# k and v with four neighbouring tokens on a partition, k^T v as 128x64 products, values as four 64x64 products at a time

## The chip, the core and the metric

The kernel runs on one core of one Trainium2 chip. The core has five engines that run their own instruction streams and wait for each other by semaphores: TensorE (matrix products; in the profile PE, and PEld for its weight loads), VectorE (DVE), ScalarE (ACT), GpSimd (POOL) and SyncE (SP, which here only issues transfers). Sixteen DMA engines move data between the memory of the chip and the core's own. The metric is the time of one execution on the device in microseconds; lower is better. Three executions of the kernel before are given, with their median.

## What is computed

Two blocks follow each other. The first is an attention without softmax, for 8 batches, 8 heads, 576 tokens and heads of 64 numbers. The second sends each of the 4608 tokens to one of eight experts.

```python
kv = np.einsum('bhsd,bhse->bhde', k, v)
out = np.einsum('bhsd,bhde->bhse', q, kv)
rms = np.sqrt(np.mean(out * out, axis=-1, keepdims=True) + 1e-06)
x = out / rms * g_norm          # then (batch, head, token, d) -> (batch*token, head*d)
...
do_compute = (x @ w_skip) > 0
e_idx = argmax(x @ w_gate);  gate_w = softmax's value there
y = gate_w * (relu(x @ w1[e_idx]) @ w2[e_idx])
out = x + y   where do_compute, else x
```

All numbers are float32. So for each batch and head a 64x64 matrix k^T v is summed over 576 tokens, and each token's q is multiplied with it.

## The kernel before

The work is in two stages. The attention stage writes x to the output tensor and finds out which expert each token needs. The expert stage gathers the tokens of one expert after another, runs the two layers, and scatters the results.

**Tokens on partitions.** `load` (L99 to L103) brings one batch of k, v or q into a tile of 128 partitions. Partition p of the lower half holds the nine neighbouring tokens 9p to 9p+8 of the even heads, the upper half those of the odd heads: `(j a) (p c) d -> (a p) j (c d)` with a = 2 and c = C = 9. A load is one DMA with pieces of 2304 bytes. `load_kv(b)` issues k and v of a batch, `load_q(b)` its q, all on the SP queue. There are three buffers for each.

**k^T v.** `state(b, third)` (L283) makes the eight heads' 64x64 sums. It runs in three thirds, each put at another place in TensorE's order. In each third six steps (u, c) are made: u is the half of the heads (four each), c the piece of nine tokens. A step is four products of 64 rows by 64 columns, one in each quarter of the TensorE array: a picks the upper or lower rows, w the left or right columns. All go to `sum_ps`, in which a is the PSUM bank. After the last third ScalarE copies the sums to `kvn`. `state_t` and `state_m` work out what w_gate and w_skip make of k^T v (nine further columns, G), so that a product with q gives logits as well; `state_s` makes `kvs`, a copy with the halves of the partitions swapped.

**Units.** The attention loop (L713) has 36 units. A unit is 256 tokens of one batch (i = 0 or 1) for one half u of the heads; the 64 tokens of a batch that are left (the ninth of each nine) are put together for four batches in units of their own (i = None). For each unit, in this order:

- `turn(n)` (L344) turns q with four TensorE transposes into `q_ps`, and ScalarE copies that to `qT`. For the left units `turn_8` does it beside other units.
- `values(n)` (L376) multiplies qT with kvn or kvs into `o_ps`, of which there are two buffers. In a usual unit eight products of 64 rows by 128 columns are made, two at a time (r is the half of the rows). In a left unit the columns too are cut in two (hf), with sixteen products of 64 by 64, four at a time. Each has 73 moving columns: 64 of k^T v and nine for the logits. TensorE needs two passes for a float32 product, which the profile records as two matmuls.
- ScalarE squares into `sq` (L398); VectorE sums the squares, `rs` (L406, `squares`); ScalarE takes the root (L413, `root`); VectorE inverts it (L420) and multiplies o_ps by it into `xl` (L423, `norm`); GpSimd adds logits and multiplies by g_norm (`finish`, L456); stores go out on the GpSimd and SP queues.

**Order.** The loop is written out by hand (`tc.manual_schedule`). In step n come turn(n+1), root(n-1), values(n), norm(n-1), squares(n); then what was put down for this step with `at`: the parts "pe" (thirds of `state` and what follows it for a batch four units ahead, L705), "late" (the routing) and "end" (loads of k and v three batches ahead and q two ahead, L706 to L709).

**Routing.** When the first 16, 26 and 36 token tiles are done, `choose`, `rank` and `number` (VectorE, with a few products) find each token's expert and slot. These stand in VectorE's order between the norms of the units.

**Start.** Loads of k, v and q of batch 0, then k and v of 1 and 2 and q of 1 (L669 to L673) go out on SP, while ScalarE's queue loads w_gate, w_skip and g_norm in six small transfers (L119 to L128). Then the parts of `state` for batch 0 run, with turn(0) after `state_t`, and the loop starts.

Of the kernel before, what the change touches and what calls it, by code (L numbers as in the profile page):

```python
# [7 lines left out]
FP32 = mybir.dt.float32  # L8
# [8 lines left out]
def kernel(  # L17
# [31 lines left out]

    nc = tc.nc
    B, H, S, D = q.shape
    DM = H * D
    N = B * S
    P = 128
    C = S // 64
    CT = 4
    NQ = 2
    NF = B // 4  # L60
    FQ = 4 * NQ + 1
# [6 lines left out]
    CAP = 384  # L68
# [3 lines left out]
    NCOL = E * CK  # L72
    ROUNDS = N // CAP
    RSPACE = 8192
    assert H == 8 and D == 64 and S == 64 * C and C == 2 * CT + 1 and B == 4 * NF and N == CAP * ROUNDS
    assert N + CAP <= RSPACE and DM == DC * 128 and NT * P == N

    keep = ctx.enter_context(tc.tile_pool(name="keep", bufs=1))
# [4 lines left out]
    kv_pool = attn.enter_context(tc.tile_pool(name="kv", bufs=3))  # L83
    q_pool = attn.enter_context(tc.tile_pool(name="q", bufs=3))
# [12 lines left out]

    kts, vts, qts = {}, {}, {}

    def load(pool, tag, src, b):  # L100
        t = pool.tile([P, 4, C, D], FP32, tag=tag, name=tag)
        nc.sync.dma_start(out=t[:, :, :, :].rearrange("p j c d -> p j (c d)"),
                          in_=src[b].rearrange("(j a) (p c) d -> (a p) j (c d)", a=2, c=C))  # L103
        return t

    def load_kv(b):
        if b < B:
            kts[b] = load(kv_pool, "k", k, b)
            vts[b] = load(kv_pool, "v", v, b)

    def load_q(b):
        if b < B:
            qts[b] = load(q_pool, "q", q, b)

    order = tc.manual_schedule()
    order.__enter__()
# [6 lines left out]
    for a in range(2):  # L123
        nc.scalar.dma_start(out=gcol[a * 64:(a + 1) * 64, :],
                            in_=g_norm.rearrange("(e o) -> e o", o=1))
# [76 lines left out]
    for w in range(2):  # L202
        nc.vector.tensor_copy(out=swap[:, w * 64:(w + 1) * 64],
                              in_=ident[:, (1 - w) * 64:(2 - w) * 64])
# [4 lines left out]
    for a in range(2):  # L209
        r = slice(a * 64, (a + 1) * 64)  # L210
# [15 lines left out]
    for lo, m in kinds:  # L226

        t = keep.tile([P, P], FP32, name=f"again{lo}_{m}")
# [43 lines left out]
    sum_ps = ps_kv.tile([P, 2, 512], FP32, name="sum_ps")[:, :, 0:2 * D].rearrange("p a (u d) -> p a u d", u=2)  # L272
# [9 lines left out]

    def state(b, third):  # L283

        kt, vt = kts[b], vts[b]
        for i in range(6 * third, 6 * third + 6):
            u, c = divmod(i, C)
            for w in range(2):
                for a in range(2):
                    r = slice(a * 64, (a + 1) * 64)  # L290
                    nc.tensor.matmul(  # L291
                        out=sum_ps[w * 64:(w + 1) * 64, a, u, :],
                        lhsT=kt[r, 2 * u + w, c, :], rhs=vt[r, 2 * u + w, c, :],
                        start=(c == 0), stop=(c == C - 1), skip_group_check=True)
        if third < 2:
            return
        kvn = kvn_pool.tile([P, 2, PK], FP32, tag="kvn", name="kvn")
        nc.scalar.copy(out=kvn[:, :, G:G + 2 * D].rearrange("p u (a d) -> p a u d", a=2), in_=sum_ps)
        kvns[b] = kvn
# [76 lines left out]
    def values(n):  # L376
        _, b, i, u = units[n]
        qT = qTs.pop(n)
        ps = ps_o.tile([P, 2, 512], FP32, tag="o", name="o_ps")

        done = turn_8(b, u, ps) if i == 0 else None
        for w in range(2):
            for a in range(2):
                cols = slice((2 * w + a) * KD, (2 * w + a + 1) * KD)
                for hf in range(1 if i is not None else 2):
                    for r in range(2):
                        rows = slice(r * 64, (r + 1) * 64)
                        if i is not None:
                            bb, to, lhsT = b, slice(0, P), qT[rows, w, a, :]
                        else:  # L390
                            bb, to = 4 * b + 2 * hf + r, slice(hf * 64, (hf + 1) * 64)
                            lhsT = qT[rows, w, hf, a * 64:(a + 1) * 64]
                        kv = kvns[bb] if w == r else kvss[bb]
                        nc.tensor.matmul(out=ps[to, r, cols], lhsT=lhsT,  # L394
                                         rhs=kv[rows, u, a * KD:(a + 1) * KD],
                                         start=True, stop=True, skip_group_check=True)
        sq = att_pool.tile([P, 2, 2, 2 * D], FP32, tag="sq", name="sq", bufs=2)
        nc.scalar.activation(out=sq[:, :, :, :], in_=heads(ps, G, G + 2 * D), func=ACT.Square)  # L398
        if done:
            done()  # L400
        ops[n] = (ps, sq)
# [276 lines left out]
    for b in range(KNOWN // S // 4 * 4, KNOWN // S):  # L678
        nc.gpsimd.dma_start(
            out=out[b * S:(b + 1) * S, :].rearrange("(p c) d -> p c d", c=C)[:, C - 1, :],  # L680
            in_=zero[:, :])
# [20 lines left out]
    for b, n in starts.items():  # L702
        if b:
            for i, part in enumerate(parts):
                at(max(n - 6 + i, (0, 0, 1, 1, 2, 3)[i]), "pe", lambda b=b, part=part: part(b))  # L705
        def loads(b=b):  # L706
            load_kv(b + 3)
            load_q(b + 2)
        at(n, "end", loads)  # L709

# [57 lines left out]
    with tc.tile_pool(name="wpool_b", bufs=2, reuse_waits="tile") as wpool_b, \  # L768
# [197 lines left out]
        rows, src = slot_rows(slice(0, NCOL), slot_pool, "")  # L966
# [37 lines left out]
        with tc.For_i(1, n_rounds, 1):  # L1004
# [8 lines left out]
                out=left[:, :].rearrange("p (r c) -> p r c", c=CK),  # L1013
# [38 lines left out]
```

## Time and profile before

| | us |
|---|---|
| three executions | 455.43, 453.71, 454.67 |
| median | 454.67 |
| the profiled execution | 461.48 |
| its span, first to last instruction | 459.6 |
| busy: TensorE / its weight loads | 400.7 / 284.0 |
| busy: VectorE / ScalarE / GpSimd | 131.4 / 94.1 / 118.4 |

The profile is of one execution, taken apart from the three. Its mean granted TensorE clock is 0.915 of full speed: in some stretches the clock was cut to one half. The costliest groups of the attention stage on TensorE are these (busy time is the union of overlapping instructions, so two groups that run at once each show it):

| line, what | records | busy us |
|---|---|---|
| L394 values, o_ps with kvn | 256 | 41.3 |
| L394 values, o_ps with kvs (at the same time) | 256 | 40.4 |
| L394 values, left units, kvn and kvs (at the same time) | 64 each | 4.7 each |
| L291 k^T v, sum_ps | 1152 | 27.4 |
| L353 transposes of q, q_ps | 128 | 24.1 |

The transfers concerned are 8 loads each of k, v and q of 1152 KB, with a median of 13.1, 13.8 and 14.9 us from issue to landing.

How to read the views that are used below. The page shows the span in 40 equal slices; a digit is the busy share of an engine in that slice in tenths, PEclk the granted clock, DMA the share of the sixteen engines. The chain of waits goes back from the last instruction: at each point it names the work that had to end for the next to start, with start, length and count. In the timeline and in the list of windows each line has a start or a stretch in us from the span's start. "x16" counts records. "64*128" is the part of the array that a product fills (rows by columns), "64x73" the moving operand.

### The profile page before, as it was taken

Reading aid. Unit: us, or ns where it says so; the run is one execution under the profiler, and the core shown is the slowest. Engines: PE = TensorE matmul, PEld = TensorE weight load, DVE = VectorE, ACT = ScalarE, POOL = GpSimd, SP = SyncE. Lnnn points to the kernel's source line nnn. Section 1 sums busy time; section 2 is a strip of 40 time slices with the busy share of each in tenths; the row PEclk is TensorE's granted clock in tenths of the full one; section 3 lists DMA queues with packets and bytes.
Section 4 is the critical chain, followed back from the end, with each engine's and each line's share of the span. In section 5 each row is a group of like instructions: output and inputs, shape, how many; then the busy total and the mean of one; then the engine's idle time right before and its main releaser. Section 6 shows DMA issues by size and latency. Waiting matters only on the chain.

```text
span 459.6 us, 8262 instructions
## 1 busy us (share of the span) xinstructions
PE 400.7 (87%) x3495; PEld 284.0 (62%) x3495; DVE 131.4 (29%) x357; ACT 94.1 (20%) x220; POOL 118.4 (26%) x185
## 2 busy tenths in 40 slices
PE   0789998998755894799999999999999999999980
PEld 0688787786645853675654764674764765856730
DVE  3132566679787552111011010110010011010010
ACT  1253574545342110010210110020110110201100
POOL 2014477444539167502001100100100101001010
PEclk9995998899675786799999999999999999999995
DMA  7899997963459999532541614425523600001000
GB/s 233 337 392 388 384 342 296 296 256 95 93 175 334 309 403 371 165 134 113 181 141 64 216 22 191 151 73 199 185 78 150 210 0 24 25 1 46 0 23 21
DMA packets 32777, 81.79 MB, mean 178 GB/s; under 512 B 3326, under 2 KB 3330, under 8 KB 32736
## 3 DMA queue, kind: packets, MB, share of 16 engines
q1 hardware_dynamic: 26656, 66.59, 41.4%
q0 software_dynamic: 4576, 14.54, 9.3%
q8 instruction: 29, 0.48, 0.4%
q10 hardware_dynamic: 1504, 0.08, 0.2%
q14 instruction: 12, 0.10, 0.1%
HBM read 66.87 MB, written 14.61 MB: 177 GB/s over the span
## 4 chain that ended last, share of the span: by engine, by line
PE 74%; DVE 13%; DMA 4%; issue 2%; ACT 2%; another core or an unknown queue 1%; POOL 0%; DVEq 0%; ACTq 0%; POOLq 0%
PE hps L888 29%; PE yps L899 27%; PE o_ps L394 6%; PE sum_ps L291 3%; PE q_ps L353 3%; DVE xl L423 3%; DMA q<-in_q_dram 2%; DVE oha_k L555 2%; PE xp L869 2%; DVE rs L406 2%; PE g_ps L320 2%; DMA wraw<-in_moe_w_gate_dram 1%; DVE bv L571 1%; DVE xt L872 1%
## 5 line engine op out<-in xcount | busy, mean ns | idle before, releaser
L888 PE MATMUL hps<-xt,w 128*128 128x288 f32 (+5 forms) x576 | 138.4, 403 | 3.7 <-issue 2.9
L899 PE MATMUL yps<-w,ht 128*32 128x128 f32 (+2 forms) x672 | 132.7, 413 | 0.0
L888 PEld LDWEIGHTS hps<-xt,w 128*128 128x128 f32 x576 | 108.9, 201 | 31.6 <-issue 5.4
L899 PEld LDWEIGHTS yps<-w,ht 128*32 128x32 f32 (+2 forms) x672 | 63.8, 145 | 66.0 <-issue 62.9
L890 ACT ACTIVATE ht<-hps 128x288 f32<-128x288 f32 (+5 forms) x72 | 28.2, 393 | 256.2 <-PE hps L888 255.0
L913 POOL DMA_INDIRECT out_dram<-xg,rows x16 | 15.8, 990 | 220.0 <-DVE xg L910 210.3
L394 PE MATMUL o_ps<-kvn,qT 64*128 64x73 f32 x256 | 41.3, 306 | 9.2 <-DVE xl L423 8.2
L394 PEld LDWEIGHTS o_ps<-kvn,qT 64*128 64x128 f32 x256 | 36.3, 213 | 15.1 <-issue 7.9
L872 DVE COPY xt<-xp 128x512 f32<-128x512 f32 x16 | 10.4, 687 | 114.2 <-PE xp L869 113.4
L910 DVE SCALAR_TENSOR_TENSOR xg<-yps,gate,xg 128x512 f32<-128x512 f32 x16 | 12.0, 750 | 107.3 <-PE yps L899 107.3
L394 PE MATMUL o_ps<-kvs,qT 64*128 64x73 f32 x256 | 40.4, 307 | 0.0
L456 POOL TENSOR_TENSOR xb<-xl,g_b 128x512 f32<-128x512 f32 x32 | 39.1, 1222 | 0.0
L291 PE MATMUL sum_ps<-v,k 64*64 64x64 f32 x1152 | 27.4, 257 | 10.7 <-DMA v<-in_v_dram 10.4
L394 PEld LDWEIGHTS o_ps<-kvs,qT 64*128 64x128 f32 x256 | 35.4, 214 | 1.0 <-ACT rs L413 1.0
L291 PEld LDWEIGHTS sum_ps<-v,k 64*64 64x64 f32 x1152 | 24.2, 167 | 14.6 <-issue 13.5
L423 DVE TENSOR_TENSOR xl<-o_ps,rs 128x584 f32<-128x584 f32 x36 | 27.6, 767 | 4.5 <-DVE rs L420 0.5
L440 POOL TENSOR_TENSOR lp<-xl 128x36 f32<-128x36 f32 x36 | 9.1, 254 | 73.2 <-DVE xl L423 73.1
L406 DVE TENSOR_REDUCE rs<-sq 128x8 f32<-128x512 f32 x36 | 24.5, 680 | 11.6 <-ACT sq L398 11.2
L398 ACT ACTIVATE sq<-o_ps 128x512 f32<-128x512 f32 x36 | 21.5, 597 | 23.8 <-PE o_ps L394 23.7
L353 PE MATMUL q_ps<-ident,q 128*128 128x128 f32 x128 | 24.1, 319 | 1.9 <-DMA q<-in_q_dram 1.9
L356 ACT COPY qT<-q_ps 128x512 f32<-128x512 f32 x32 | 18.8, 587 | 28.9 <-PE q_ps L353 28.8
L353 PEld LDWEIGHTS q_ps<-ident,q 128*128 128x128 f32 x128 | 16.6, 161 | 4.7 <-DMA q<-in_q_dram 2.3
(143 smaller groups left out, 251.1 us busy)
## 6 DMA issues: line engine op xcount, KB each, us to landing
w<-in_moe_w_dram SPq DMA_DIRECT2D x16, 2048.0 KB, 8.5
k<-in_k_dram SPq DMA_DIRECT2D x8, 1152.0 KB, 13.1
v<-in_v_dram SPq DMA_DIRECT2D x8, 1152.0 KB, 13.8
q<-in_q_dram SPq DMA_DIRECT2D x8, 1152.0 KB, 14.9
out_dram<-xb SPq DMA_DIRECT2D x8, 512.0 KB, 6.3
out_dram<-xb POOLq DMA_DIRECT2D x8, 512.0 KB
out_dram<-x SPq DMA_DIRECT2D x2, 256.0 KB, 6.5
out_dram<-x POOLq DMA_DIRECT2D x2, 256.0 KB
```

Of the source, the lines that this page charges most:

```text
L291: nc.tensor.matmul(out=sum_ps[w * 64:(w + 1) * 64, a, u, :], lhsT=kt[r, 2 * u + w, c, :], rhs=vt[r, 2 * u + w, c, :], start=(c == 0), stop ...
L353: nc.tensor.transpose(out=ps[:, w, :, hf, :], in_=qts[b][:, 2 * u + w, c:c + 2, :], identity=ident[:, :])
L356: nc.scalar.copy(out=qT[:, :, :, :].rearrange("p w a t -> p (w a t)"), in_=ps[:, :, :, :, :].rearrange("p w a h t -> p (w a h t)"))
L394: nc.tensor.matmul(out=ps[to, r, cols], lhsT=lhsT, rhs=kv[rows, u, a * KD:(a + 1) * KD], start=True, stop=True, skip_group_check=True)
L398: nc.scalar.activation(out=sq[:, :, :, :], in_=heads(ps, G, G + 2 * D), func=ACT.Square)
L406: nc.vector.tensor_reduce(out=rs[:, :, :], in_=sq[:, :, :, :].rearrange("p r w (a d) -> p r (w a) d", a=2), axis=AX.X, op=ALU.add)
L423: nc.vector.tensor_tensor(out=xl[:, :, :, :].rearrange("p r w (a k) -> p r (w a) k", a=2), in0=ps[:, :, 0:2 * PK].rearrange("p r (h k) -> ...
L456: nc.gpsimd.tensor_tensor(out=xb[:, :, 4 * u * D:(4 * u + 4) * D].rearrange("p r (w x) -> p r w x", w=2), in0=xl[:, :, :, G:G + 2 * D], in ...
L888: nc.tensor.matmul(out=hps[:, cols], lhsT=w_sb[r][0][:, dc, f * P:(f + 1) * P], rhs=xt[:, dc, cols], start=(dc == 0), stop=(dc == DC - 1))
L890: nc.scalar.activation(out=ht[:, f, cols], in_=hps[:, cols], func=ACT.Relu)
L899: nc.tensor.matmul(out=yps[q * m:(q + 1) * m, 0:n], lhsT=ht[:, f, off:off + m], rhs=w_sb[r][1][:, f, q * n:(q + 1) * n], start=(f == 0), s ...
L913: ins = nc.gpsimd.indirect_dma_start(out=cut_rows(m)[:, :], out_offset=bass.IndirectOffsetOnAxis(ap=rows[:, col:col + 1], axis=0), in_=x, ...
```

## The change

**k and v.** The first 512 tokens of each head lie with four neighbouring tokens on each of 128 partitions, so a piece is 1024 bytes, and a head fills all the partitions. The last 64 tokens of each head are loaded apart into a second tile, even heads on the lower 64 partitions and odd heads on the upper, in two DMAs with pieces of 256 bytes. A load of k or v is three DMAs. q is loaded as before.

**k^T v.** For each half u of the heads there are five steps c in place of nine: four with 128 tokens (products of 128 rows by 64 columns; two fill the array), and one with the 64 tokens apart (products of 64 by 64; four fill it). The thirds have 3, 3 and 4 of the ten steps. The order within a step is a, then w.

**Values.** A usual unit too cuts its columns in two and makes sixteen products of 64 by 64.

```diff
+    KC = 4
...
-    def load(pool, tag, src, b):
-        t = pool.tile([P, 4, C, D], FP32, tag=tag, name=tag)
-        nc.sync.dma_start(out=t[:, :, :, :].rearrange("p j c d -> p j (c d)"),
-                          in_=src[b].rearrange("(j a) (p c) d -> (a p) j (c d)", a=2, c=C))
-        return t
-
     def load_kv(b):
-        if b < B:
-            kts[b] = load(kv_pool, "k", k, b)
-            vts[b] = load(kv_pool, "v", v, b)
+        if b == B:
+            return
+        for x, (ts, src) in enumerate(((kts, k), (vts, v))):
+            t = kv_pool.tile([P, H, KC, D], FP32, tag=f"kv{x}", name=f"kv{x}")
+            nc.sync.dma_start(out=t[:, :, :, :].rearrange("p h c d -> p h (c d)"),
+                              in_=src[b, :, 0:P * KC, :].rearrange("h (p c) d -> p h (c d)", c=KC))
+            r = kv_pool.tile([P, 4, D], FP32, tag=f"kvr{x}", name=f"kvr{x}")
+            for a in range(2):
+                nc.sync.dma_start(
+                    out=r[a * 64:(a + 1) * 64, :, :],
+                    in_=src[b, :, P * KC:S, :].rearrange("(j a) p d -> a p j d", a=2)[a])
+            ts[b] = (t, r)
...
     def state(b, third):
 
-        kt, vt = kts[b], vts[b]
-        for i in range(6 * third, 6 * third + 6):
-            u, c = divmod(i, C)
-            for w in range(2):
-                for a in range(2):
-                    r = slice(a * 64, (a + 1) * 64)
-                    nc.tensor.matmul(
-                        out=sum_ps[w * 64:(w + 1) * 64, a, u, :],
-                        lhsT=kt[r, 2 * u + w, c, :], rhs=vt[r, 2 * u + w, c, :],
-                        start=(c == 0), stop=(c == C - 1), skip_group_check=True)
+        (km, kr), (vm, vr) = kts[b], vts[b]
+        for i in ((0, 1, 2), (3, 4, 5), (6, 7, 8, 9))[third]:
+            u, c = divmod(i, KC + 1)
+            for a in range(2):
+                r = slice(a * 64, (a + 1) * 64)
+                for w in range(2):
+                    h = 4 * u + 2 * w + a
+                    if c < KC:
+                        lhsT, rhs = km[:, h, c, :], vm[:, h, c, :]
+                    else:
+                        lhsT, rhs = kr[r, 2 * u + w, :], vr[r, 2 * u + w, :]
+                    nc.tensor.matmul(out=sum_ps[w * 64:(w + 1) * 64, a, u, :], lhsT=lhsT, rhs=rhs,
+                                     start=(c == 0), stop=(c == KC), skip_group_check=True)
...
-                for hf in range(1 if i is not None else 2):
+                for hf in range(2):
+                    to = slice(hf * 64, (hf + 1) * 64)
                     for r in range(2):
                         rows = slice(r * 64, (r + 1) * 64)
-                        if i is not None:
-                            bb, to, lhsT = b, slice(0, P), qT[rows, w, a, :]
-                        else:
-                            bb, to = 4 * b + 2 * hf + r, slice(hf * 64, (hf + 1) * 64)
-                            lhsT = qT[rows, w, hf, a * 64:(a + 1) * 64]
+                        bb = b if i is not None else 4 * b + 2 * hf + r
+                        lhsT = qT[rows, w, a, to] if i is not None else \
+                            qT[rows, w, hf, a * 64:(a + 1) * 64]
```

In the same edit the body of `load` moves into `load_q`, and the call of `load_kv(b + 3)` becomes `load_kv(min(b + 3, B))`.

## The prediction

> **What bounds the kernel now.** I read the page's slices first, for what limits each stretch; then the chain of waits, for what a saved instruction is worth; then the TensorE timeline, for the step of each kind of product; last the SP queue from the start.
>
> ```profile
> PE   0789998998755894799999999999999999999980
> DVE  3132566679787552111011010110010011010010
> PEclk9995998899675786799999999999999999999995
> DMA  7899997963459999532541614425523600001000
> ```
>
> A slice is 11.5 us. Attention fills the first 13, the experts the rest, which the change doesn't touch. The busy times by stretch (columns: TensorE, weight loads, VectorE, ScalarE, GpSimd, then clock, DMA share, GB/s) divide the attention:
>
> ```profile
> 17.50:75.00 57.50, 53.93 (x944) 45.83 (x944) 25.40 (x54) 29.63 (x68) 24.78 (x45) 0.88 1.04 378
> 95.00:118.00 23.00, 19.89 (x403) 16.08 (x401) 19.91 (x51) 13.73 (x32) 11.14 (x20) 1.00 0.42 130
> 118.00:129.00 11.00, 9.99 (x81) 8.54 (x82) 7.74 (x26) 3.47 (x8) 4.65 (x8) 0.53 0.38 89
> ```
>
> TensorE is the bound to about 95 us. From there VectorE shares it and, by the chain, mostly has it: norms plus the routing of finished tokens. From 118 to 129 us TensorE, at half clock, is the bound again. The chain prices the two groups that are changed:
>
> ```profile
> 41.95 1.92 PE o_ps L394 x16
> 43.87 1.49 PE sum_ps L291 x48
> 48.68 1.05 PE o_ps L394 x16
> 50.29 0.86 PE sum_ps L291 x48
> 80.97 1.18 PE o_ps L394 x32
> 104.79 1.44 DVE oha_k L555 x4
> ```
>
> A unit of values (x16 records, each product being two) takes 1.05 us at full and 1.92 us at half clock. The x32 line is the leftover unit, which already does four 64x64 products at a time: 1.18 us at half clock for the same work. So the trace holds the new form. At full clock the timeline shows its step:
>
> ```profile
> 66.05 0.27 PE L394 MATMUL o_ps<-kvn,qT 64*128 64x73 f32 x1
> 66.17 0.27 PE L394 MATMUL o_ps<-kvn,qT 64*128 64x73 f32 x1
> ...
> 66.50 0.27 PE L394 MATMUL o_ps<-kvn,qT 64*128 64x73 f32 x1
> 66.70 0.93 PE L291 MATMUL sum_ps<-v,k 64*64 64x64 f32 x48
> 75.22 0.22 PE L394 MATMUL o_ps<-kvn,q 64*64 64x73 f32 x1
> 75.28 0.23 PE L394 MATMUL o_ps<-kvn,q 64*64 64x73 f32 x1
> ```
>
> A pair of 64x128 products steps by 0.11 us, a set of four 64x64 by 0.066. The start is set by loads:
>
> ```profile
> 0.75 0.46 SPq L102 DMA_DIRECT2D k<-in_k_dram  x1
> 1.28 0.49 SPq L102 DMA_DIRECT2D v<-in_v_dram  x1
> 7.15 0.37 SPq L102 DMA_DIRECT2D q<-in_q_dram  x1
> 17.61 1.12 PE L353 MATMUL q_ps<-ident,q 128*128 128x128 f32 x4 [1.88 <-DMA q<-in_q_dram]
> ```
>
> The list of waits adds why the first q goes out only at 7.15 us:
>
> ```profile
> SPq L102 <- DMA wraw<-in_moe_w_gate_dram: 5.4, 1, 5.4
> ```
>
> q has no data in common with w_gate. In the trace's DMA records both count on the same semaphore, and the SP and ScalarE loads use eight in rotation: each load waits until the eighth before it has landed.
>
> [...] from the last pair at 66.50 to the first 64x64 product at 66.70 is 0.20 us, 0.09 over a step, and the first matmul of the group lasts 267 ns against the usual 218, so 0.14 us a switch. [...] The trace's median packets: 2304 B in 93 ns, 2048 B in 84, 256 B in 15.
>
> **Values.** 32 units go from 16 records (8 pair steps) to 32 records (8 steps of four). At half clock 1.92 - 1.18 = 0.74 us is saved. At full clock 8 x (0.11 - 0.066) = 0.35; the chain's x24 line of that form is 0.61 us, so x32 is near 0.74 and the saving 0.31: I take 0.31. On the chain stand 19 such units, four wholly at half clock (from 22.61, 35.80, 41.95 and 123.57 us) and fifteen near full clock: 4 x 0.74 + 15 x 0.31 = 7.6 us, a ceiling. What is late next: from 59 to 63 and from 70 to 75 us the chain passes values, sq on ScalarE, then qT, then xl on VectorE, and back through the two o_ps buffers; there values count only once in two units. Other paths stand a few tenths behind elsewhere. I take four fifths, 6.1 us. The units off the chain, mostly after 95 us, give nothing while VectorE has the end; if it didn't they'd give up to 13 x 0.31 = 4 more.
>
> **k^T v.** Per batch 72 products in 18 sets of four, so 36 steps in two records each, become 32 of 128x64 in 16 pairs and 8 of 64x64 in 2 sets: 32 + 4 = 36 steps again. Step before: 0.86 us for 12, start included; between starts 0.058 us in the trace's records. The 128x64 form with 64 moving columns isn't in the trace. Its nearest row is in the experts: 128x64 with 256 moving columns runs in column pairs, 96 records in 11.0 us, 0.23 us a pair, so both tiles do multiply at once. [...] I take 0.058, since the 64x64 sets load two column tiles over the same rows in that time. So no gain from the count of steps. The 64 tokens apart come after four chunks of each half, between 128x64 products: two mode switches more in the second third, one in the last, 3 x 0.14 = 0.42 us a batch at full clock, double at half. On the chain lie the thirds of batches 1 to 6: by their clock 0.28, 0.84, 0.42, 0.28, 0.5 and 0.28, sum 2.6 us; four fifths as above, 2.1 us lost. [...]
>
> **Loads.** A tensor of a batch was 512 packets of 2304 B, 512 x 93 / 16 = 2.98 us of 16 DMA engines. Now 1024 of 1024 B and 512 of 256 B: on a line through the packets above, 45 ns each for the first, so 2.88 + 0.48 = 3.36 us, 0.39 more, twice a batch. From batch 2 on this is hidden: q of batch 2 landed at 42.1 us and is turned at 54.3; k and v of batch 3 landed by 39.1, used at 50.2. At the start there is no cover. v of batch 1 landed at 23.6 and is used at 24.5. A k or v load is now three issues on SP, so v goes from the second to the fourth. Before, k was counted second of the eight and v eighth; v then comes tenth and waits for the first k load, as its predecessor waits for w_gate. That puts v, with its rest and q behind it, at some 6.5 us instead of 1.28, behind the small g_norm loads: in the records q's packets began only at 12.9 us, when those were nearly done. Without v among them I expect those done 2 us sooner: the stream restarts at 10.9. Until v of batch 1 it carries 3.36 + 2.98 + 3.36 + 3.36 = 13.1 us in place of 8.9, plus the 1.8 us left to landing before (12.9 + 8.9 to 23.6): 25.8 us against a use at 24.5, 1.3 us late. Bounds: 0.3 if v isn't held (the packets alone), 3.3 if the stream still restarts at 12.9. I take 1.3. The later issues (seven loads a batch instead of three) stay in order before the out stores on SP; a store waits for GpSimd anyway (65.9 us of SP's waiting), so 0.
>
> **Sum.** -6.1 + 2.1 + 1.3 = -2.7 us. The profiled execution took 461.48 us (span 459.6 and 1.9 around it), so 458.8. The median of the runs shown is 454.67, 6.8 us less, which half-clock stretches may well explain; without them the values save 0.31 where I counted 0.74 and a switch costs half, nearly the same net. Forecast 454.67 - 2.7 = 452.0.
>
> **Rivals.** (a) Covers are better than thought: v not held, all of 7.6 real, some units after 95 us too: -7.6 + 2.1 + 0.3, and up to -1 more: 448.5. For it: TensorE sits at nine tenths to 75 us. Against: VectorE has the end by 100 us. (b) No change: the stream restarts late (3.3) and the o_ps loop gives only half of the values (-3.8), with 1.6 for switches: +1.1, 455.8; with half of each doubt 454.5. (c) Slower, one mechanism: the 128x64 pairs' weight loads follow one another[...]. On the chain lie some 130 pair steps, a third of them at half clock, so 170 by weight[...]. For it: no row shows that form with few moving columns. Against: the 64x64 sets. (d) Slower by the clock: TensorE, less busy from 95 us, is cut to half clock there as from 118 to 129 us; a unit costs some 4 us of it instead of VectorE's 3.3, for five units or more, and as much again after: 458.
>
> **Chances.** Forecast 0.45, (a) 0.12, (b) 0.13, (c) 0.15, (d) 0.15. What a measurement can tell from no change is 0.5%, 2.3 us. The forecast's own range, 449.5 to 454, lies two thirds below 452.4: 0.30 faster, 0.15 same. With (a): faster 0.42. With most of (b): same 0.25. The rest, (c), (d) and 0.03 of (b): slower 0.33. Range 447.5 to 460, which cuts the tails of (c) and (a).
>
> **What would show it.** Values as x32 records near 0.75 us at full clock; 128x64 pairs of sum_ps stepping by 0.058[...]; a gap of a tenth around the rest products; v of batch 0 issued near 6.5 us; sum_ps of batch 1 waiting for v; clock from 95 to 130 us. Wrong if o_ps falls and the end of attention, near 148 us, doesn't move.

## The result, and the profile after

| | executions | median us | ratio to before, 95% interval |
|---|---|---|---|
| before | 4 | 454.19 | |
| changed | 4 | 460.74 | 1.0136 [1.0096, 1.0176] |

The change makes the kernel slower by some 6.5 us; the forecast was 452.0, faster than before. In some executions, the one profiled with this result among them, the expert stage waits some 15 us more at one place; such executions are left out of every ratio, and the lines of the changed kernel below come from a second profile of the same kernel (460.60 us, span 458.8), taken in the first experiment. There k^T v is L306, turn L366, values L406, the loads of the 64 tokens apart L113, those of the other k and v L109, q L121.

The slices of the page, 11.5 us each:

```profile
PE   0566977898653887589999999999999999999980
PEclk9998998899775797889999999999999999999995
DMA  6999999995449999642441614424523600001000
```

From the second slice to the tenth TensorE was at seven to nine tenths and is now at five to nine; the DMA engines, which let up in the seventh and ninth slice before, are now at nine tenths in all from the second to the ninth. The table by stretch has the same columns as before (TensorE, weight loads, VectorE, ScalarE, GpSimd, clock, DMA share, GB/s):

```profile
17.50:75.00 57.50, 44.04 (x952) 35.17 (x952) 24.00 (x51) 28.99 (x66) 21.85 (x40) 0.97 1.09 328
95.00:118.00 23.00, 19.11 (x442) 14.82 (x438) 19.79 (x51) 13.88 (x32) 12.00 (x21) 1.00 0.66 220
118.00:129.00 11.00, 8.22 (x136) 6.51 (x136) 9.13 (x26) 3.98 (x9) 4.67 (x8) 0.69 0.40 93
```

To 75 us TensorE was busy for 53.93 us before and is for 44.04 now, in part because its clock was higher (0.97, before 0.88). It idles 13.5 of the 57.5 us, and the engines behind it have done no more work. The DMA engines carry 328 GB/s where they carried 378. So something else now sets the pace. (The profile of the kernel before is of an execution of 461.48 us, 7 us above its median, so the pair of profiles shows where the waits are and not the loss itself; that is taken up near the end.) The parts of the chain of waits between 17 and 47 us that show the new forms and the first loss (start, us, what):

```profile
30.45 8.61 DMA q<-in_q_dram
39.05 0.14 issue
39.19 1.09 PE q_ps L366 x4
...
42.69 1.04 PE sum_ps L306 x24
...
44.53 0.67 PE o_ps L406 x32
45.20 1.12 PE sum_ps L306 x32
```

A unit of values is x32 records in 0.67 us, where x16 took 1.05, both at full clock: the products did get cheaper. The thirds of k^T v that hold the 64 tokens take 1.04 and 1.12 us, where each took 0.86. And q of batch 1, which SP issued at 30.45 us behind the new loads (16.96 before), lands at 39.1 us (before at 32.9, in a second profile at 33.3) and holds TensorE for 3.1 us. Further on, the chain of the same execution leaves TensorE altogether:

```profile
53.21 9.98 DMA out_dram<-xb
63.33 1.18 POOL xb L468
...
67.60 9.88 DMA out_dram<-xb
77.53 0.48 issue
78.01 1.18 POOL xb L468
...
83.17 0.23 POOL lg L458
83.42 0.29 DVE mx L498
```

A store of finished tokens takes 10 us from issue to landing beside the loads. `xb`, the tile of finished tokens, has two buffers, so GpSimd waits, the logits (`lg`) come late, and VectorE's routing (`mx`, the row maximum) waits for them; the norms are queued behind it on VectorE. In the kernel before, the chain between 50 and 84 us was mostly TensorE's. The waits behind it, GpSimd's in the attention stage and VectorE's from 60 to 100 us (us in all, times, longest), neither of which is in the profile before (a second one of that kernel has a single wait of 0.9 us for a store):

```profile
POOL xb L468 <- DMA out_dram<-xb: 10.1, 2, 6.9
...
DVE mx L498 <- POOL lg L458: 3.2, 1, 3.2
```

The 10 us are not new: the store whose landing can be told took 6.8 us in the profile before and 11.6 in a second one. New is when it starts. One half of an `xb` tile is stored from GpSimd's queue, the other from SP's, in order with the loads there. Before, SP was ready first; a set of three loads took it from 59.73 to 65.17 us:

```profile
59.02 0.61 SPq L473 DMA_DIRECT2D out_dram<-xb  x1
59.73 0.55 SPq L102 DMA_DIRECT2D k<-in_k_dram  x1
60.33 2.62 SPq L102 DMA_DIRECT2D v<-in_v_dram  x1
63.04 2.13 SPq L102 DMA_DIRECT2D q<-in_q_dram  x1
```

Now a set of seven takes from 55.15 to 67.51, and the half on SP goes out 8.4 us after GpSimd's half of the same tile (4.6 and 10.9 for the stores before and after this one):

```profile
59.17 0.66 POOL L484 DMA_DIRECT2D out_dram<-xb  x1 [0.30 <-POOL xb L468]
...
55.15 0.62 SPq L109 DMA_DIRECT2D kv<-in_k_dram  x1
55.86 4.62 SPq L113 DMA_DIRECT2D kvr<-in_k_dram  x2
60.52 1.86 SPq L109 DMA_DIRECT2D kv<-in_v_dram  x1
62.43 4.43 SPq L113 DMA_DIRECT2D kvr<-in_v_dram  x2
66.96 0.55 SPq L121 DMA_DIRECT2D q<-in_q_dram  x1
67.60 0.71 SPq L485 DMA_DIRECT2D out_dram<-xb  x1
```

Issued at 59.2 us, it would by the same 10 us have landed near 69 (an estimate), before GpSimd asked for the buffer at 71.1. SP's list of waits says the same: before, all eight stores on SP waited there for GpSimd to finish `xb`; now four do.

```profile
SPq L473 <- POOL xb L456: 65.9, 8, 12.7
SPq L485 <- POOL xb L468: 27.3, 4, 12.5
```

### The profile page after: what moved, and what is told of

Its sections match the earlier page's. It is cut to its first block, busy times and chain, and to the rows that moved or that the text cites. A ratio compares the mean times of both kernels' runs of the same rounds, so it can differ in the third digit from the quotient of the medians.

```text
span 472.8 us, 8314 instructions
## 1 busy us (share of the span) xinstructions
PE 385.3 (82%) x3495; PEld 267.4 (57%) x3495; DVE 131.8 (28%) x357; ACT 94.0 (20%) x220; POOL 117.4 (25%) x185
## 4 chain that ended last, share of the span: by engine, by line
PE 69%; DVE 12%; SPq 5%; another core or an unknown queue 5%; DMA 4%; issue 2%; ACT 1%; POOL 0%; DVEq 0%; ACTq 0%; POOLq 0%
PE hps L900 28%; PE yps L911 26%; SPq L113 4%; PE o_ps L406 3%; PE sum_ps L306 3%; PE q_ps L366 3%; DVE xl L435 2%; DVE oha_k L567 2%; PE xp L881 2%; DMA q<-in_q_dram 2%; DVE rs L418 2%; DMA kv<-in_k_dram 1%; DMA xg<-out_dram,src 1%; PE g_ps L333 1%
## 5 line engine op out<-in xcount | busy, mean ns | idle before, releaser
L306 PE MATMUL sum_ps<-kv,kv 128*64 128x64 f32 x512 | 25.0, 249 | 21.0 <-DMA kv<-in_v_dram 18.0
L468 POOL TENSOR_TENSOR xb<-xl,g_b 128x512 f32<-128x512 f32 x32 | 39.1, 1221 | 4.3 <-DMA out_dram<-xb 4.3
L406 PE MATMUL o_ps<-kvn,qT 64*64 64x73 f32 x512 | 27.0, 248 | 10.2 <-DVE xl L435 10.2
L306 PEld LDWEIGHTS sum_ps<-kv,kv 128*64 128x64 f32 x512 | 20.5, 157 | 25.5 <-DMA kv<-in_v_dram 17.4
L406 PEld LDWEIGHTS o_ps<-kvn,qT 64*64 64x64 f32 x512 | 21.7, 148 | 16.8 <-DVE xl L435 8.5
L406 PE MATMUL o_ps<-kvs,qT 64*64 64x73 f32 x512 | 26.2, 248 | 0.2 <-issue 0.2
L369 ACT COPY qT<-q_ps 128x512 f32<-128x512 f32 x32 | 18.8, 586 | 33.5 <-PE q_ps L366 33.3
L366 PE MATMUL q_ps<-ident,q 128*128 128x128 f32 x128 | 22.7, 305 | 3.0 <-DMA q<-in_q_dram 2.7
L406 PEld LDWEIGHTS o_ps<-kvs,qT 64*64 64x64 f32 x512 | 21.1, 148 | 0.4 <-issue 0.4
L366 PEld LDWEIGHTS q_ps<-ident,q 128*128 128x128 f32 x128 | 15.7, 154 | 5.3 <-issue 3.3
## 6 DMA issues: line engine op xcount, KB each, us to landing
kv<-in_k_dram SPq DMA_DIRECT2D x8, 1024.0 KB, 10.9
```

The source lines that it names most:

```text
L306: nc.tensor.matmul(out=sum_ps[w * 64:(w + 1) * 64, a, u, :], lhsT=lhsT, rhs=rhs, start=(c == 0), stop=(c == KC), skip_group_check=True)
L366: nc.tensor.transpose(out=ps[:, w, :, hf, :], in_=qts[b][:, 2 * u + w, c:c + 2, :], identity=ident[:, :])
L369: nc.scalar.copy(out=qT[:, :, :, :].rearrange("p w a t -> p (w a t)"), in_=ps[:, :, :, :, :].rearrange("p w a h t -> p (w a h t)"))
L406: nc.tensor.matmul(out=ps[to, r, cols], lhsT=lhsT, rhs=kv[rows, u, a * KD:(a + 1) * KD], start=True, stop=True, skip_group_check=True)
L468: nc.gpsimd.tensor_tensor(out=xb[:, :, 4 * u * D:(4 * u + 4) * D].rearrange("p r (w x) -> p r w x", w=2), in0=xl[:, :, :, G:G + 2 * D], in ...
```

## The experiments

They ran on five chips, on which the kernel before has medians from 445.51 to 457.38 us, so a ratio counts and not a time. Numbers of lines shift by a few between the kernels.

**The same two kernels again.** The kernel before, and the changed one twice, on two chips:

> The kernel before, unchanged, for a second profile beside the ones that follow. All theories: 454 us, no difference. Of interest is the time that lies between the last values (near 144 us in the first profile) and the first long run of expert products (184.7 us there): if the waits of VectorE for a late TensorE signal in there (3.7 and 2.8 us in the first profile) differ from run to run, they are no part of the change.

> The changed kernel, unchanged. All theories: near 460.7 us. Loads theory (the longer stream of k and v loads, and three issues in place of one, make the first 40 us later and eat what values save): q of batch 1 lands near 38.8 us and values of unit 4 start near 45.6 us against 41.9 before. Rival (the loss lies in the expert stage): the last values start within 0.5 us of e1 and the difference is made after them.

> The changed kernel as it is, on the same chip for comparison: all theories 1.010 to 1.018, with the waits of GpSimd for stores and of VectorE for the logits' maximum as before, 3 to 10 us and 1 to 4 us.

Measured: 1.0005 [0.9981, 1.0029], 1.0136 [1.0069, 1.0204] and 1.0181 [1.0128, 1.0233]. The loss is firm.

**Each part alone.** First values as four 64x64 products, with loads and k^T v as before:

```diff
-                for hf in range(1 if i is not None else 2):
+                for hf in range(2):
+                    to = slice(hf * 64, (hf + 1) * 64)
```

> Only values as four 64x64 products; k and v loaded and multiplied as before. Loads theory: the saving on TensorE is kept, 449 us, 4 to 7 us faster than before. Rival V (the shorter values only make room for waits of VectorE and for a lower clock, so nothing comes out at the end): 454, no change. Rival W (values' new form is itself what costs): slower than before by 3 us or more.

Then k and v alone (the new loads and k^T v, values in pairs), twice:

> Only the k and v part: loads with four tokens a partition and the last 64 apart, and 128x64 products; values as before. Loads theory: all of the loss and none of the gain, 464 us or more, slower than the changed kernel. Rival V: as the changed kernel, 460.7. Rival W: 455, no slower than before.

> The changed kernel with values as before (64x128 products in pairs): the k and v part alone, whose earlier run had but one undisturbed execution, 463.4 us. If the k and v part alone explains the loss (longer loads and 0.43 us of mode switches a batch): ratio 1.010 to 1.020 and, with fewer TensorE instructions than before, no stops. If the two parts share it: 1.003 to 1.008.

Measured: values alone 1.0187 [1.0118, 1.0256], some 9 us slower, where a gain was expected. That refuted the first theory, by which only the loads lost time. For k and v alone there are three executions to compare: 463.44 us beside a median of 454.12, and 452.81 and 449.74 beside 445.06, so 1.1 to 2.1% slower, without an interval. Values alone lose, k and v alone by these three too, and the two together lose less than the sum. The chain of the kernel with values alone shows a new kind of piece; from 60 to 82 us it has:

```profile
66.15 0.33 PE sum_ps L291 x20
66.48 1.02 issue
67.50 0.68 PE sum_ps L291 x25
...
70.95 0.40 PE o_ps L393 x10
71.34 2.63 issue
73.97 0.87 PE o_ps L393 x17
```

"issue" is time in which TensorE waited for nothing that the profile shows, and it falls in the middle of a group: 20 records of one third, a pause of 1.02 us, then the rest. In this kernel's waits of the weight loads from 20 to 125 us it comes first:

```profile
PEld o_ps L393 <- issue: 16.0, 26, 4.1
PEld sum_ps L291 <- issue: 11.3, 10, 2.8
```

against 4.8 and 4.6 us in the kernel before (its second profile; 6.1 and 3.1 in the first). Number all of TensorE's records in order of start, weight loads, matmuls and its sequencer's, and measure a pause from the start of one record to the start of the next: every pause over 0.7 us without a wait stands before a record whose number is 193 over a multiple of 256: 705, 1473, 1985, 2241 and on, nine of them, 19.0 us in sum. The page lists what could have that period:

```profile
q8 instruction: 33, 0.54, 0.5%
```

This queue moves instructions in packets of 16 KB (0.54 MB in 33); 33 here, 29 before and in the changed kernel, 25 with k and v alone. Values cut in four add 1024 records (32 units of eight more products, each with two loads and two matmuls), which is four blocks of 256; k^T v over 128 rows takes four away. The packets change by the same four each way, so one packet goes with one block of 256 records. That TensorE stops where such a block comes too late became theory F; the following runs test it.

**Without the loads.** The kernel before, and the one with values alone, without the loads of k and v from batch 3 and of q from batch 2 on (the earlier tiles are used again, so tokens, their experts and the expert stage are others; only the attention stage can be compared):

```diff
     def load_kv(b):
-        if b < B:
+        if 2 < b < B:
+            kts[b], vts[b] = kts[b - 3], vts[b - 3]
+        elif b < B:
```

> The kernel before without the loads of k and v from batch 3 and of q from batch 2 on; the first tiles are used again, so the outputs of those batches are of other tokens. TensorE's stops at every 256th instruction (the fetch of instructions waits behind the loads) should be gone; there is about one of 2 us in e1, so 450 to 453. It is the partner of e8.

> As e7, with values as four 64x64 products. Fetch theory (e3 loses 19 us to stops at 256-instruction borders because TensorE runs through its instructions faster than they are fetched past the loads): without the loads the stops go, and the saving shows: 4 to 7 us under e7. Rival W (the 64x64 form itself, or the clock, costs): 5 us or more over e7, as e3 over e1.

Measured: whole times of 810.81 and 811.07 us say nothing, since the tokens crowd on few experts. The start of ScalarE's squares of a unit serves as a clock of the stage: from unit 0 to unit 12, 35.9 us with products in pairs and 33.8 with four at a time. So 2.1 of 12 x 0.31 = 3.7 us arrive. From unit 0 to 35 it is 109.8 and 111.2: lost again. The pauses were none with pairs and 9.6 us in six with four at a time, five of them after the last load had landed, where none were forecast. So full DMA engines aren't needed for them, but with all loads their sum is twice as large (19.0).

**Early or late units.** Values in four only from unit 22 on, where loads are nearly over, or only up to unit 21:

```diff
-                for hf in range(1 if i is not None else 2):
+                split = i is None or n >= 22
+                for hf in range(2 if split else 1):
```

> The kernel before, with values as four 64x64 products only from unit 22 on (12 of the 32 full units), loads and k^T v as before. Theory F (TensorE runs out of fetched instructions at borders of 256 instructions while the loads fill the DMA engines): the loads have landed by then, so fewer than 3 us of stops in the attention stage in all, and the saving of 0.3 us a unit shows where TensorE is late last: 1 to 3 us faster, ratio 0.994 to 0.998. Theory F2 (the fetch itself is slower than TensorE's new pace, loads or not): stops of 1 us or more appear in the stretch from 100 to 145 us, as in the run without loads, and take the saving back: ratio 0.999 to 1.004. Theory G (values save nothing because VectorE has the end there): no stops, ratio 1.000.

> The kernel before, with values as four 64x64 products only up to unit 21 (20 of the 32 full units), loads and k^T v as before: the other part of the same edit. Theory F and F2: the stops of 1 to 3 us at borders of 256 instructions come back between 25 and 100 us, 10 us or more in sum, and the time is 5 to 9 us over the kernel before: ratio 1.011 to 1.020. Theory G (values' products alone neither gain nor lose, and the loss of all 32 units came from something else, such as the clock): ratio 0.995 to 1.003.

Measured: late 1.0018 [0.9956, 1.0079], pauses 2.8 us in two, both before unit 22, as in the kernel before. Early 1.0129 [1.0040, 1.0217], seven pauses, 14.0 us. The early units bring the loss of values alone; the late ones add none that can be told, and gain nothing either, which fits theory G (VectorE has the end there).

**All instructions moved by 128 places.** Values alone, with 64 small bfloat16 products, two records each, ahead of the first k^T v:

```diff
+    for _ in range(64):
+        nc.tensor.matmul(out=g_ps[0:64, 0:64], lhsT=ones[:, 0:64], rhs=ones[:, 0:64], start=True, stop=True)
```

> The kernel before with all values as four 64x64 products, and 64 small bfloat16 products (128 records) on TensorE ahead of the first k^T v, while it has nothing to do. They move every later instruction by 128 places. If the stops come from the fetch of blocks of 256 instructions: they stay at record numbers 193 over a multiple of 256 (705, 1473, 1985 and so on), which are now other products of other units, and none is left at the old products (which have the numbers 833, 1601, 2113 now). If the stops belong to something in the code (a wait that the records don't show): they move with the products to 833, 1601, 2113. Time in both cases as for values alone, ratio 1.012 to 1.020.

Measured: 1.0207 [1.0140, 1.0274]. Pauses at 1217, 1473, 1729, 2497, 2753, 3521 and 4033, again all at 193 over a multiple of 256, 15.0 us in sum; none at 833, 1601 or 2113. They belong to the block and not to the code. The records of the DMA packets show how, worked out here for some runs (us):

| kernel | from one border to the start of the next fetch | from that start to the next border, where TensorE paused | pauses over 0.6: number, sum |
|---|---|---|---|
| before (again) | 2.8 to 4.1 up to 70 us | 2.4, 2.6 | 2, 2.8 |
| values alone | 3.7 to 4.2 from 42 to 75 us | 2.2 to 2.6 | 9, 19.0 |
| values alone, no loads | 0 to 1.3 in most blocks, up to 4.5 in others | 2.2 to 2.5 | 6, 9.6 |
| changed | 3.1 to 5.0 from 47 to 72 us | 2.4 to 2.6 | 3, 4.4 |

After each border one block was fetched, and the next border was passed no sooner than 2.2 us after that fetch began (the packet itself took 1.1). Beside the loads a block of values alone that ended in a pause therefore cost some 3.8 + 2.4 = 6.2 us. Six of its blocks went from 42.4 to 79.9 us, 6.24 each (5.9 to 6.5): TensorE ran at the pace of its instructions. The kernel before took 6.4 a block from 24.5 to 75.7 us, close to that. In the changed kernel fetches start later: the blocks that ended in a pause took 6.7, 7.5 and 7.0 us (to 60.2, 67.7 and 74.8 us), and in another execution 9.8 and 7.3.

**Number and size of the packets.** The kernel before with each k and v load as three transfers, first in whole pieces of 2304 bytes, then cut in pieces of 1024, 1024 and 256 (shown); products as before:

```diff
+        for c0, c1 in ((0, 4), (4, 8), (8, 9)):
+            nc.sync.dma_start(
+                out=t[:, :, c0:c1, :].rearrange("p j c d -> p j (c d)"),
```

> The kernel before, but each k and v load issued as three DMAs over the heads, with pieces of 2304 bytes as before; products as before. It has the changed kernel's number of issues and rotation of semaphores, and nothing of its packets. If the number of issues is what makes q of batch 1 land late: landing near 38 us as in e2 and 459 or more. If the packets are: q lands within 2 us of e1's, and 455 to 456.

> The kernel before, but each k and v load cut by tokens into three DMAs with pieces of 1024, 1024 and 256 bytes: the changed kernel's packets, bytes and number of issues, with products as before. Loads theory: q of batch 1 lands near 38.8 us as in e2, and the time is that of the k and v part alone less its mode switches: 460 to 463. If the 128x64 products are what costs in e4: 455.

The same cut for batches 0 to 2 alone, and for 3 to 7 alone:

> The kernel before with k and v of batches 0 to 2 alone loaded in pieces of 1024, 1024 and 256 bytes (three transfers a tensor), the later ones in one as before; all products as before. If the small pieces cost at the start, where no load is ahead of its use: unit 3 two to three us later than before and the whole loss of the fully cut loads, ratio 1.007 to 1.012. If they cost through the long run of transfers beside the rest: 0.999 to 1.003.

> The same with k and v of batches 3 to 7 alone in the small pieces. If the cost is at the start: ratio 0.998 to 1.003, start as before. If the small pieces cost through the length of the stream (other transfers, instructions' fetch among them, held up to 75 us and beyond): 1.005 to 1.012, with more stops of TensorE at the borders of 256 instructions than the 2 to 3 us of before.

Measured: three transfers 1.0012 [0.9979, 1.0045]; small pieces 1.0107 [0.9988, 1.0226]; only at the start 1.0039 [1.0013, 1.0065]; only later 1.0016 [0.9984, 1.0047]. The number of issues costs nothing that shows; the small pieces do, at the start by 1.7 us, later by too little to tell. SP shows the same difference: the 56 issues of loads take it 34.7 us in sum with whole pieces, and its half of each store goes out with GpSimd's; with all cut they take 77.5 us (83.2 in the changed kernel; before, 24 issues took 44.8), and the half on SP is 4.5 to 6.6 us late three times. What holds SP in an issue the trace doesn't show. All cut, packets took 50.7 ns (1024 B) and 18.1 (256 B), and q of batch 1 landed at 36.0 us; with the start alone cut, at 36.1. In the changed kernel they are 55.8 and 19.1 ns, so a tensor takes (1024 x 55.8 + 512 x 19.1) / 16 = 4.18 us against 512 x 97.1 / 16 = 3.11 before. The transfers of the changed kernel from 17.5 to 75 us, in the view of the DMA engines:

```profile
DMA packets 18533, 18.84 MB, mean 328 GB/s; under 512 B 5727, under 2 KB 15913, under 8 KB 18524
```

The same line of the kernel before, run again beside it, shows half the packets and a fifth more data in the same time:

```profile
DMA packets 9585, 22.76 MB, mean 396 GB/s; under 512 B 360, under 2 KB 360, under 8 KB 9574
```

**q of batch 1 earlier.** The changed kernel with q of batch 1 loaded ahead of k and v of batch 2, and the kernel before with that and late values in four:

```diff
     load_kv(1)
-    load_kv(2)
     load_q(1)
+    load_kv(2)
```

> The changed kernel with q of batch 1 loaded ahead of k and v of batch 2 at the start, nothing else. Theory A (the smaller packets of k and v delay q of batch 1, landing at 38.8 us in the changed kernel, and unit 3 waits for it): q of batch 1 lands near 28 to 30 us, unit 3's squares start at 37 to 38 us instead of 41.6, and some 3 to 4 us of that remain at the end: ratio to the kernel before 1.004 to 1.008. Theory B (what k^T v and values do on TensorE later is the cost, the start is made up for): unit 3 is earlier but unit 16 is not, ratio stays at 1.012 to 1.015. Theory A has a limit: k and v of batch 2 land 3 us later, near 40 us, and if their first product is then late, the gain is lost there.

> The kernel before, with q of batch 1 loaded ahead of k and v of batch 2 and values as four 64x64 products from unit 22 on. If both hold: unit 3's squares start 1 to 3 us sooner than the 36.4 us of before, and the late values add 1 to 3 us: ratio 0.988 to 0.996. If the early q only moves the wait to k and v of batch 2: the same as the late values alone, within 0.002.

Measured: 1.0135 [1.0057, 1.0213] and 1.0010 [0.9944, 1.0076]. q landed at 30.4 us, and the wait went to the load behind it; the chain of the changed kernel with q first:

```profile
26.71 10.99 DMA kv<-in_v_dram
37.70 0.14 issue
37.84 0.92 PE sum_ps L306 x24
```

Unit 3 came at 41.0 us in place of 41.6 (38.4 in a third profile of the changed kernel). All eight tensors are wanted by then, and another order doesn't shorten their sum. The combination gives no more than late values alone: no version was found that beats the kernel before.

**A third buffer for the stores.** The changed kernel with three `xb`, for which `qT` gave up its third buffer:

```diff
-    xb_pool = attn.enter_context(tc.tile_pool(name="xb", bufs=2))
+    xb_pool = attn.enter_context(tc.tile_pool(name="xb", bufs=3))
...
-        qT = att_pool.tile([P, 2, 2, P], FP32, tag="qT", name="qT")
+        qT = att_pool.tile([P, 2, 2, P], FP32, tag="qT", name="qT", bufs=2)
...
-    zero = setup.tile([64, DM], FP32)
-    nc.gpsimd.memset(zero[:, :], 0.0)
+    zero = xg0[0:64, 0, :]
+    nc.gpsimd.memset(zero, 0.0)
```

> The changed kernel with three buffers for xb, the finished tokens on their way to memory, instead of two (room made by two instead of three buffers for qT, and by taking the zeros from a tile that is used later). In the changed kernel's trace GpSimd waits 3.2 and 6.9 us for a store of xb, which takes 10 us from issue to landing beside the loads, and VectorE's first maximum of the logits then waits 3.2 us for GpSimd. Theory S (this wait carries a part of the loss): GpSimd's wait for stores goes, VectorE's maximum waits under 0.5 us, attention ends 2 to 3 us sooner and the ratio is 1.005 to 1.010. Theory F (TensorE's supply of instructions, 7.4 us a block of 256 from 60 to 82 us, is what is late): the waits go, the stops of TensorE stay at 4 to 6 us, ratio 1.011 to 1.016.

Measured: 1.0174 [1.0128, 1.0220], beside 1.0181 for the changed kernel on the same chip, where GpSimd waited 12.6 us for stores and VectorE 3.8 for the maximum. With three buffers both waits are gone (the half of the stores on SP is still 4.5 to 9.4 us late), and nothing is gained: the chain returns to TensorE and meets the pauses. That `qT` has one buffer less shows in no wait of ScalarE in this run.

```profile
59.90 0.34 PE o_ps L406 x2
60.24 1.26 issue
61.50 0.73 PE o_ps L406 x30
...
66.42 0.67 PE sum_ps L306 x17
67.08 1.24 issue
68.32 0.45 PE sum_ps L306 x7
...
72.54 0.84 PE sum_ps L306 x22
73.38 1.42 issue
74.81 0.60 PE sum_ps L306 x10
```

Each splits a group in two (x2 + x30, x17 + x7, x22 + x10). So two paths lie close to each other: stores through GpSimd to VectorE's routing, and TensorE's instructions. Unit 17 starts at 83.3 us with three buffers, at 83.3 and 82.0 in two profiles of the changed kernel. Theory F fits (three pauses, 4.6 us in sum; the ratio lies just over its 1.016). Theory S named a true wait that decides nothing while the other path is as late.

## Why the prediction was wrong, point by point

**Values: right on TensorE, wrong at the end.** The unit takes 0.67 us in the chain (0.74 was expected), so a saving of 0.38 a unit at full clock. The step that failed is "I take four fifths, 6.1 us". Its list of what is late next held `sq`, `qT`, `xl` and the `o_ps` buffers, and left out what feeds TensorE itself: the new form has twice the records in two thirds of the time. The chain before had shown "issue" of about a microsecond in two places, which the text passed over. Alone, the part measured some +9 us instead of -6.1: 19.0 us of pauses where the kernel before has 2.8.

**k^T v: right.** 12 steps of 128x64 products take 0.92 us, as 12 of four 64x64 products took 0.93, so rival (c) is out: by its 170 steps, 2.7 / 170 = 0.016 us more a step would have undone the forecast's gain (an estimate). For the switches between 128x64 and 64x64 products 0.42 us a batch was taken; the two thirds that hold the 64 tokens give 1.04 + 1.12 - 2 x 0.86 = 0.44, or 0.15 for each of the three switches. What no step asked is the effect on records: this part takes away 1024, as many as values add. That fits the pauses: 4.4 us in the whole change, 19.0 in values alone, none in k and v alone.

**Loads: too cheap, and not hidden.** "45 ns each" for 1024 B was 55.8, so a tensor costs 1.07 us more in packet time and not 0.39 (packets overlap a little, by the DMA shares of 1.09 and 1.04; the clock then sees 4.18 / 1.09 - 3.11 / 1.04, some 0.8 us, an estimate). A straight line between packets of 256 and 2304 bytes (15 and 93 ns) was no good measure for this full stream. v of batch 1 landed at 26.4 us (25.8 forecast), in part by luck: the DMA engines were full again from 10 us on (share 0.96 from 10 to 11 us) and not from 10.9, which paid for a part of the longer packets. And "From batch 2 on this is hidden" failed three times. q of batch 1 comes behind k and v of batch 2 and was never priced: it had 1.8 us of cover in the first profile (landed 32.9, turned at 34.7), 0.4 in the second (33.3, 33.7), and became 3.1 us late. For the further issues on SP the sum had "a store waits for GpSimd anyway", "so 0": now the half of a store on SP waits for the loads ahead of it, 4.6 to 10.9 us, and with 10 us of its own it fills both `xb` buffers. And instruction blocks travel through the same engines (q8, 0.4% of their time): 6.7 to 7.5 us for those that made TensorE pause.

**Where the loss stands.** The run with late values is the kernel before up to unit 21, and its profiled execution took 455.57 us. Its units 3, 12, 17, 22 and 35, by the start of their squares, come at 38.0, 62.5, 74.5, 95.6 and 139.8 us; the changed kernel's at 41.6, 65.9, 83.3, 100.3 and 144.5 (on another chip). After unit 35 both need the same 314 us. By these two profiles the loss is in the attention stage, and some 5 us of it stand from unit 22 on; between units 12 and 17, where stores are late and TensorE pauses, the gap grows to 8.8 us and then closes in part. The first profile of the kernel before hides this: its unit 35 came at 145.6 us. The prediction's own sign of being wrong, `o_ps` shorter and the end of attention no earlier, did appear.

**The start doesn't simply add.** On another chip the changed kernel waited 1.2 us for q of batch 1 in place of 3.1, and unit 3 came at 38.4 us, not 41.6; yet unit 22 came at 100.0 against 100.3 and unit 35 at 144.1 against 144.5. What is slow from 50 to 83 us, stores and instructions, swallowed the better start. So the 6.5 us can't be divided into a share for each: that the pauses make the loss of values alone is shown, what each path takes of the whole change's loss is not. It also stays open whether k and v alone, which have no pauses but the wait for stores (0.9 us of `mx` in one profile, 2.3 in another), would gain by a third `xb` buffer, and whether stores that don't queue behind the loads on SP would help: neither was tried.

**Right besides:** the number of issues on SP alone costs nothing (three transfers a load in whole pieces: 1.0012); units off the chain give nothing (late values: 1.0018); the clock from 95 to 129 us is no worse (1.00 and 0.69, 1.00 and 0.53 before), so rival (d) is out; that a less busy TensorE would get a lower clock was the author's estimate and is not shown (busy for 19.11 of 23 us from 95 us on, 19.89 before). Two prices of rivals were mis-added, without effect on the rest: midway between the forecast and (b) lies 453.9 and not 454.5, and five units of 0.7 us twice over put (d) at 459 and not 458. No rival named what happened, though the side of the sum that (b) doubted, the values' saving, is the one that went.

## What to carry to other kernels

In this kernel a block of 256 TensorE instructions cost some 6.2 us beside full loads in packets of 2304 bytes, and 6.7 to 7.5 beside the smaller packets. So before making an engine's instructions smaller and more, compare its time for such a block with what the block costs to fetch beside the transfers of that stage; an "issue" piece that splits a group in the chain (1.02 us between x20 and x25) was the sign here that this floor was near. With the stream of loads full (DMA share 1.09), the longer packet list wasn't hidden by loading ahead: q of batch 1 held TensorE for 3.1 us, stores took 10 us to land, blocks of instructions that ended in a pause took 6.7 to 7.5, and the half of a store that SP issued behind the loads went out as much as 10.9 us late. And if a wait is taken away and nothing is gained (1.0174 beside 1.0181 with three `xb`), read the chain again: here a second path lay right behind it.

## What the runs showed of the hardware that was not expected

- TensorE stopped at borders of 256 instructions, 0.6 to 4.3 us at a time, with nothing in the waits but "issue". One block was fetched after each border; blocks that ended in a pause cost 5.9 to 6.5 us beside full loads of 2304-byte packets (values alone, 42 to 80 us) and 6.7 to 7.5, in one case 9.8, beside those of 1024 and 256 bytes. Without loads the fetch started 0 to 1.3 us after the border in most blocks; two such blocks took 3.6 and 3.7 us. What delays the start can't be seen: the trace shows when a fetch moves, not when it was asked for.
- A packet of 1024 bytes took 50.7 ns cut out of whole rows and 55.8 in the new layout; why the second is slower wasn't tried.
- Small pieces lengthened the issue of loads on SP (56 issues: 77.5 and 83.2 us in sum, with whole pieces 34.7), and what SP issued after them was late by as much as 10.9 us.
